# A new order of the same instructions on every engine: gateloop attention and squared-ReLU FFN

## Chip, cores, metric

One NeuronCore of a Trainium2 chip. The metric is the device time of one execution in microseconds (us). A "profile" is one recorded execution; its span leaves out about 1.8 us of the device time. In the profiles PE is the matrix engine, DVE the vector engine, ACT the scalar engine and POOL the general one; SP issues most DMA transfers (394 of 400 in the profile before). A "q" behind a name (SPq) is that engine's sequencer. The granted clock is what the profile records as PE's clock, as a share of the full one (1.00 is full).

## The reference, cut to what matters

```
for t in range(S):                              # S = 768 steps, 4 batches x 8 heads, head size 48
    new_re = ar * S_re - ai * S_im              # complex gate, |a| limited to 0.999
    new_im = ar * S_im + ai * S_re
    kv = np.einsum('bhd,bhe->bhde', k[:, :, t], v[:, :, t])
    S_re, S_im = (new_re + kv, new_im)
    y[:, :, t] = np.einsum('bhd,bhde->bhe', q[:, :, t], S_re)
...
h = np.maximum(x @ w_in, 0.0)                   # x: 3072 x 384, w_in: 384 x 2048
return (h * h @ w_out).astype(np.float32)       # w_out: 2048 x 384, weights given in float64
```

## The kernel before

The tokens are worked off in 12 groups of 256 (two chunks, a and b, of 128). A group's gates become products on DVE and ACT ("o" steps), PE makes scores, values and states from them ("a" and "b" steps), and two matrix products follow ("F", then "T" or "Z"). The float64 weights are decoded on DVE ("D" steps). The whole order is written down by hand in one string; DVE, PE, SP and ACT are given their instructions in the order in which the string names the steps (in the profile DVE stood still for 2.91 us before the second mask of group 1, at 122.20 us, and D10, which the string puts next on DVE, began behind it at 123.34 us):

```
    work = {
        "o": lambda gi, k: operands_of[gi][k](),
        "a": lambda gi, k: chunks_of[gi][0][k](),
        "b": lambda gi, k: chunks_of[gi][1][k](),
        "g": fill_gaps,
        "F": first_product,
        ...
        "T": block_of_second,
        "E": end_of_second,
        ...
        "s": store,
        "f": fetch,
        "D": weights,
        ...
        "l": load_parts,
        "v": load_values,
    }
    ...
    by_hand = {mybir.EngineType.DVE, mybir.EngineType.PE, mybir.EngineType.SP,
               mybir.EngineType.Activation}
    with tc.manual_schedule(engines=by_hand):
        follow(FRONT)
```

The second product of group 0 sums in two tiles of the pool `py`, the one of group 1 in a tile of the pool `pa`:

```
    ffn = ctx.enter_context(tc.tile_pool(name="ffn", bufs=2))
    pa = ctx.enter_context(tc.tile_pool(name="pa", bufs=1, space=PSUM))
    py = ctx.enter_context(tc.tile_pool(name="py", bufs=2, space=PSUM))
    ...
    def block_of_second(i, f):
        if f == 0:
            if i:
                both = pa.tile([C, HH, NP, C], F32, tag="a", name="o_ps").rearrange(
                    "p b x t -> p (b x t)")
            for b in range(GC):
                o_of[i, b] = both[:, b, 0:DM] if i else py.tile([P, DM], F32, tag="y", name="o_ps")
        for b in range(GC):
            second_product(i, b, [f])
```

The results are copied to output tiles (`bufs=2` of `ffn`), and stored:

```
    def end_of_second(i, b):
        out_of[i, b] = ffn.tile([P, DM], F32, name="o")
        nc.scalar.copy(out=out_of[i, b], in_=o_of[i, b])

    def store(i, b):
        nc.sync.dma_start(out=in_turn(out, groups[i][b]), in_=out_of[i, b])
```

And the scores of the next group take the same `py` and `pa` tiles again, so they cannot start before those copies are done:

```
        def scores():
            ...
            ys = tiles["y"] = [py.tile([P, NP, C], F32, tag="y", name="y") for _ in range(2)]
            ps = tiles["ps"] = pa.tile([C, HH, NP, C], F32, tag="a", name="a_ps")
```

## Time and profile before

| | before |
|---|---|
| median of the first 3 runs | 707.13 us (706.68 to 709.1) |
| PE starts its unbroken run (T0.0) | 125.7 us |
| end of the products of groups 0 and 1 | 188.5 us |
| first product of group 2 starts (F2.0) | 204.6 us |
| last matmul ends / span of the profile | 699.4 / 706.7 us |

Up to T0.0 DVE decides, later PE: from 72 to 102 us DVE is busy for 28.8 of 30 us, from 126 to 189 PE for 63.0 of 63. Between 188.5 and 204.6 us, called the hole below, PE has no bulk work: group 1's products are done and group 2's scores, masks and values must come first. The chain of waits of the kernel before over the hole (start us, length us, what), with the small pieces left out, reads

```profile
188.47 0.33 PE tp L866 x3
188.80 1.03 PE y L851 x32
189.83 2.01 PE a_ps L859 x32
...
191.86 1.23 DVE a L478
...
198.81 1.15 DVE a L478
...
202.28 2.21 DMA x<-x
```

The state products and the scores (PE y, then PE a_ps) follow on the products within 0.4 us, the two masks (DVE a) are 7 us apart, and the hole ends with a small DMA on which F2.0 waits.

### The profile page before, as it was taken

Reading aid. Unit: us, or ns where it says so; the run is one execution under the profiler, and the core shown is the slowest. Engines: PE = TensorE matmul, PEld = TensorE weight load, DVE = VectorE, ACT = ScalarE, POOL = GpSimd, SP = SyncE. Lnnn points to the kernel's source line nnn. Section 1 sums busy time; section 2 is a strip of 40 time slices with the busy share of each in tenths; the row PEclk is TensorE's granted clock in tenths of the full one; section 3 lists DMA queues with packets and bytes.
Section 4 is the critical chain, followed back from the end, with each engine's and each line's share of the span. In section 5 each row is a group of like instructions: output and inputs, shape, how many; then the busy total and the mean of one; then the engine's idle time right before and its main releaser. Section 6 shows DMA issues by size and latency. Waiting matters only on the chain.

```text
span 706.7 us, 12470 instructions
## 1 busy us (share of the span) xinstructions
PE 625.0 (88%) x4955; PEld 549.8 (78%) x4955; DVE 523.9 (74%) x916; ACT 380.6 (54%) x684; POOL 13.0 (2%) x49
## 2 busy tenths in 40 slices
PE   0007859999989999999999999999999999999995
PEld 0006638776668998988989989988989988999895
DVE  3999997979898697786696795895885975972130
ACT  6547684583636745646547458357258267350330
POOL 3000000000000000000000000000000000000000
PEclk9999977999999999999999999999999999999998
DMA  6678853505207016017034152161161170110101
GB/s 163 133 123 141 144 130 102 178 19 89 68 30 110 5 29 135 2 51 112 26 75 64 32 101 34 41 102 22 41 107 18 45 108 13 30 22 2 29 1 28
DMA packets 46148, 47.75 MB, mean 68 GB/s; under 512 B 6016, under 2 KB 40960, under 8 KB 46080
## 3 DMA queue, kind: packets, MB, share of 16 engines
q1 hardware_dynamic: 45600, 46.46, 33.6%
q8 instruction: 41, 0.67, 0.4%
q10 hardware_dynamic: 480, 0.39, 0.2%
q14 instruction: 27, 0.22, 0.1%
HBM read 36.18 MB, written 4.72 MB: 58 GB/s over the span
## 4 chain that ended last, share of the span: by engine, by line
PE 73%; DVE 13%; DMA 7%; ACT 2%; SPq 2%; issue 1%; DVEq 0%
PE h_ps L939 27%; PE o_ps L1016 23%; PE a_ps L859 6%; PE o_ps L955 6%; DVE pr L478 3%; PE y L851 3%; PE y L885 3%; DMA raw<-in_feat_dram 3%; DVE ab L478 3%; PE add L903 2%; PE tp L866 2%; DMA words<-in_moe_w_in_dram 2%; DMA vt<-in_vtok_dram 2%; SPq L815 2%; DVE room L478 1%
## 5 line engine op out<-in xcount | busy, mean ns | idle before, releaser
L939 PE MATMUL h_ps<-x,w 128*128 128x256 f32 x1152 | 258.1, 383 | 4.8 <-DMA x<-x 2.7
L939 PEld LDWEIGHTS h_ps<-x,w 128*128 128x128 f32 x1152 | 219.5, 192 | 36.4 <-ACT h L944 3.3
L944 ACT ACTIVATE h<-h_ps 128x512 f32<-128x512 f32 x96 | 57.5, 599 | 130.3 <-PE h_ps L939 127.6
L1016 PE MATMUL o_ps<-w,h 128*128 128x192 f32 x640 | 110.6, 329 | 0.0
L1016 PEld LDWEIGHTS o_ps<-w,h 128*128 128x128 f32 x640 | 103.6, 190 | 1.6 <-issue 0.5
L478 DVE TENSOR_TENSOR pr<-ab 128x384 f32<-128x384 f32 (+2 forms) x168 | 66.4, 413 | 6.0 <-ACT ab L743 1.7
L478 DVE TENSOR_TENSOR a<-a_ps,mask 128x1024 f32<-128x1024 f32 x24 | 29.4, 1224 | 54.8 <-PE a_ps L859 54.6
L866 PE MATMUL tp<-ident,qk 128*128 128x128 f32 x120 | 22.5, 300 | 50.0 <-DVE qk L478 34.9
L945 ACT ACTIVATE h<-h 128x512 f32<-128x512 f32 x96 | 60.6, 631 | 3.0
L866 PEld LDWEIGHTS tp<-ident,qk 128*128 128x128 f32 x120 | 14.8, 150 | 56.6 <-issue 37.2
L1016 PE MATMUL o_ps<-w_sum,mix 128*128 128x192 f32 x320 | 56.0, 329 | 0.0
L478 DVE TENSOR_TENSOR mix<-h 128x256 f32<-128x256 f32 x40 | 16.9, 422 | 48.2 <-ACT h L945 47.9
L1016 PEld LDWEIGHTS o_ps<-w_sum,mix 128*128 128x128 f32 x320 | 51.6, 190 | 1.1 <-issue 0.5
L478 DVE TENSOR_TENSOR ab<-pr 128x192 f32<-128x192 f32 (+1 forms) x180 | 45.8, 277 | 4.6
L478 DVE TENSOR_TENSOR qk<-ab,qk 128x768 f32<-128x768 f32 x48 | 44.9, 956 | 0.9
L669 ACT ACTIVATE qk<-raw 128x768 f32<-128x768 f32 x24 | 36.8, 1534 | 10.6 <-DMA raw<-in_feat_dram 6.5
L955 PE MATMUL o_ps<-w,h 128*128 128x384 f32 x128 | 42.2, 487 | 0.3 <-ACT x L894 0.3
L859 PE MATMUL a_ps<-qk 48*128 48x128 f32 x576 | 41.3, 293 | 0.0
L859 PEld LDWEIGHTS a_ps<-qk 48*128 48x128 f32 x576 | 36.5, 199 | 4.6 <-issue 4.2
L669 ACT ACTIVATE ab<-raw 128x768 f32<-128x768 f32 x24 | 35.7, 1577 | 2.4 <-DVE qk L478 2.4
L955 PEld LDWEIGHTS o_ps<-w,h 128*128 128x128 f32 x128 | 24.2, 190 | 16.3 <-ACT x L894 0.5
L669 ACT ACTIVATE room<-z 128x768 f32<-128x768 f32 x24 | 36.5, 1555 | 0.0
(103 smaller groups left out, 790.4 us busy)
## 6 DMA issues: line engine op xcount, KB each, us to landing
raw<-in_feat_dram SPq DMA_DIRECT2D x44, 288.0 KB
words<-in_moe_w_out_dram SPq DMA_DIRECT2D x8, 768.0 KB
last<-qk SPq DMA_DIRECT2D x72, 64.5 KB
vt<-in_vtok_dram SPq DMA_DIRECT2D x24, 192.0 KB
out_dram<-o SPq DMA_DIRECT2D x24, 192.0 KB
raw<-in_feat_dram SPq DMA_DIRECT2D x132, 32.0 KB
words<-in_moe_w_in_dram SPq DMA_DIRECT2D x16, 192.0 KB
words<-in_moe_w_in_dram SPq DMA_DIRECT2D x32, 96.0 KB
```

Source lines behind the costliest of these rows:

```text
L478: nc.vector.tensor_tensor(out=out, in0=in0, in1=in1, op=op)
L669: nc.scalar.activation(out=out.rearrange("p c j n -> p c n j"), func=AF.Copy, in_=in_.rearrange("p c (n j) -> p c n j", j=L), **kwargs)
L815: nc.sync.dma_start(out=last[gi % 2][at, :, :, 0:C + 1], in_=qk[pads(hh), :, :, g, 0:C + 1])
L851: nc.tensor.matmul(ys[p_ % 2][crossed(hh, p_), p_ // 2], lhsT=states[b][1 - c_seq % 2][rows(hh), c, p_], rhs=operand(c, p_, rows(hh)), sta ...
L859: nc.tensor.matmul(ps[:, hh, p_], lhsT=operand(2 + c, p_, rows(hh)), rhs=operand(c, p_, rows(hh)), start=(c == RE), stop=(c == IM))
L866: nc.tensor.transpose(tp[:, g], operands[gi][:, 2 + c, b, g, 0:C], ident)
L885: nc.tensor.matmul(tiles["y"][p_ % 2][crossed(hh, p_), p_ // 2], lhsT=v[:, at:at + ROWS], rhs=tiles["am"][:, hh, p_], start=(first and p_ ...
L939: nc.tensor.matmul(ps[:, j], lhsT=w1[:, g, (2 * f + j) * P:(2 * f + j + 1) * P], rhs=x_of[i][:, g], start=(g == 0), stop=(g == NG - 1))
L944: nc.scalar.activation(out=h, in_=h_ps[i, f], func=AF.Relu)
L945: nc.scalar.activation(out=h, in_=h, func=AF.Square)
L955: nc.tensor.matmul(o_of[i, b], lhsT=tokens_of(i, f, b)[:, j], rhs=w2[:, k], start=(k == 0), stop=(k == NFB - 1))
L1016: nc.tensor.matmul(to, lhsT=x(k)[:, j], rhs=factor(z)[:, 2 * k + j], start=(z in (0, 1, 3) and k == j == 0), stop=(k == KH // 2 - 1 and j ...
```

## The change

The order string was replaced by one that a longer search over a replay of the kernel had found, with two steps' durations corrected in that replay. The same 1082 steps stand in both strings and the tiles are the same. The diff is the string alone. Its lines around the end of the products of groups 0 and 1, the rest cut:

```diff
     FRONT = (
-        "l0.0 M0 v1 f0 v0 o0.0 l0.1 o0.3 o0.1 o0.4 o0.5 o0.7 o0.2 M1 D0 f1 o0.10 o0.8 o0.9 "
-        "o0.11 W0 o0.6 o0.12 o0.15 o0.22 f2 W1 o0.13 o0.16 o0.14 l1 W2 o0.17 D1 o0.18 f3 o0.19 "
...
-        "l3 o2.16 F1.7 T1.0 H1.7 o2.17 T1.1 D15 o2.18 T1.2 o2.19 T1.3 T0.7 o3.6 o2.20 o3.0 T1.4 "
-        "E0.0 E0.1 s0.0 s0.1 o3.3 o3.1 a2.1 o2.21 T1.5 t0 o3.4 o3.2 t1 T1.6 o3.5 t2 a2.2 T1.7 "
-        "o3.7 o3.10 a2.3 t3 E1.0 E1.1 s1.0 a2.0 o3.8 s1.1 o3.9 a2.5 a2.4 a2.6 o3.11 a2.8 a2.7 "
...
+        "l0.0 M0 v0 v1 f0 o0.0 l0.1 o0.3 o0.1 o0.4 o0.5 o0.7 o0.2 M1 o0.8 D0 f1 o0.9 o0.10 W0 "
+        "o0.11 o0.6 o0.22 D1 f2 o0.12 W1 o0.13 o0.15 o0.14 f3 W2 l1 o0.16 o0.17 W3 D2 f4 o0.18 "
...
+        "D14 o3.1 o3.2 T1.5 o3.4 D15 a2.2 T0.6 o3.5 a2.3 T1.6 a2.4 t0 t1 T1.7 t2 T0.7 E1.0 o3.7 "
+        "E1.1 s1.0 s1.1 o3.10 a2.8 t3 E0.0 E0.1 s0.0 a2.0 o3.8 s0.1 a2.9 o3.9 b2.1 a2.5 b2.2 "
...
```

After, group 1's come first, group 0's last block T0.7 is the last product of all, and E0 stands right before the scores a2.0.

## The prediction

> **What bounds the kernel now.** I read the page first: busy time of each engine, then the 40 slices.
>
> ```profile
> span 706.7 us, 12470 instructions
> PE 625.0 (88%) x4955; PEld 549.8 (78%) x4955; DVE 523.9 (74%) x916; ACT 380.6 (54%) x684; POOL 13.0 (2%) x49
> ...
> PE   0007859999989999999999999999999999999995
> ...
> DVE  3999997979898697786696795895885975972130
> ```
>
> PE is the largest user, but the first ten slices (17.7 us each) belong to DVE: PE starts late and has holes while DVE is at 9. From slice 12 on PE is full. So the kernel has two regimes. To find the border I cut the span into windows at places where PE's work changes (columns: window, length, busy us and instructions of PE, PEld, DVE, ACT, POOL, granted clock, DMA share, GB/s).
>
> ```profile
> 0.00:48.00 48.00, 0.47 (x1) 0.18 (x1) 34.47 (x59) 25.72 (x39) 6.80 (x25) 1.00 0.73 148
> 48.00:72.00 24.00, 16.16 (x172) 13.66 (x172) 23.41 (x29) 18.82 (x35) 0.51 (x2) 0.93 0.68 118
> 72.00:102.00 30.00, 19.41 (x85) 15.59 (x85) 28.82 (x51) 20.65 (x38) 0.00 (x0) 0.95 0.69 148
> 102.00:120.00 18.00, 16.53 (x165) 13.59 (x165) 15.72 (x21) 8.99 (x20) 0.52 (x2) 0.61 0.42 111
> ...
> 126.00:189.00 63.00, 62.99 (x239) 43.05 (x241) 57.49 (x81) 36.57 (x63) 0.58 (x2) 1.00 0.38 93
> 189.00:205.00 16.00, 11.41 (x231) 9.96 (x224) 13.34 (x21) 8.63 (x18) 0.00 (x0) 0.99 0.12 36
> 205.00:700.00 495.00, 493.01 (x3990) 449.49 (x3989) 346.96 (x655) 258.35 (x467) 4.61 (x18) 1.00 0.27 50
> ```
>
> Three things are to be seen. From 126 to 189 and from 205 to 700 us PE is busy without a hole; between them it misses 4.6 us. A busy PE need not be a fast one, so I took the spacing of matmul ends from the chain of waits: 216 ns for a 256-column one, 162.5 ns for 192 columns, 322 ns for 384, 62 ns for the scores (a_ps), and so on. Those spacings times the counts make 495 us minus 8.9 us for the last stretch: PE runs at its own pace there, and what it loses is mostly 0.2 us each time it goes from the 48- or 64-row matmuls to the full ones. True waits in that stretch are in PE's own list of waits from 204 us on:
>
> ```profile
> PE y L851 <- DMA last<-qk: 1.4, 2, 0.9
> PE h_ps L939 <- DMA x<-x: 1.2, 1, 1.2
> ```
>
> Third, PE begins its unbroken run at 125.67 us, with the first second-product block of group 0 (T0.0):
>
> ```profile
> 125.67 8.01 PE o_ps L955 x24
> 133.68 12.95 PE h_ps L939 x60
> ```
>
> All that PE does later is fixed in amount. So the end is: the start of T0.0, plus fixed matmul time, plus the hole at 189 to 205, plus the few waits, plus the 7 us tail (last copy and store). A new order of the same instructions can only move the first, third and fourth term.
>
> [...]PE idled 7.26 us before 102, the granted clock in 102 to 120 was 0.61, and 24 score matmuls took 2.94 us there and 1.61 us at 120. [...]DVE sat still 2.91 us before one masking step (scores not ready) with a weight decode standing behind it. [...]
>
> **The change, part by part.** The plan has the same 1082 steps before and after; nothing is added or removed, 911 DVE instructions are the same. So I add DVE durations along both orders, since DVE leads until T0.0. From the groups by form: a decode D is 0.558+0.959+0.563+0.959+0.958 = 4.00 us; a group's operand steps (o) sum to 27.7 us; a mask (a.5, b.5) 1.22; a state update 1.7 to 2.2. In the order before, the last operand step of group 1 (o1.20) ends at DVE sum 87.4, and the trace has it at 100.0: DVE had lost 12.6 us to waits, nearly all before 23.4 us, and then ran without a gap. Sums of the two orders, in us:
>
> - o0.20 (operands of group 0 ready): 35.7 before, 39.7 after, as decode D1 now stands before it.
> - o1.20 (group 1): 87.4 before, 81.1 after, as D4 to D7 are moved behind.
> - second mask of group 1 (b1.5), which opens T0.0: 106.7 before, 102.7 after.
> - D15, the last decode: 151.1 before, 160.6 after.
>
> So DVE work ahead of T0.0 shrinks by 4.0 us. Against it stand costs that the sums do not show:
>
> (a) The value loads v0 now go ahead of the first weights f0: two more issues of about 0.75 us, so D0, which already waited 1.30 us for f0, starts about 1.5 us later. (b) D1 now stands right after o0.11, at DVE sum 10.5, or about 24 us. Its words landed only about 27.2 us (ACT's first reader of them, L590, started at 27.25 after waiting 2.59 us for that DMA). DVE therefore stands until 27.2 or so, where before it went on at 23.4: a loss of up to 3.8 us, (a) included; 2.5 to 3.8 as SP may issue a little earlier. (c) PE comes to group 0's scores cold and now does the state sums (add, 1.95 us cold) first; b0.5 then stands behind the scores (3.8 us cold), and I count 0 to 2 us of DVE waiting. Sum: 4.0 - 3.2 - 1.0 = about 0, within -2 to +1.5.
>
> PE's own chain tells the same stretch from the other side. In the new order F0.5 waits for D5, whose sum is 85.1; with 12.6 + 3.2 + 1.0 of waits it ends at 102. After it PE must do, in order, F0.5 to F0.7 (3 x 2.6), a1's scores 3.0, its sums 1.1 and values 1.0, b1's scores 3.0, mask 1.2, values and sums 2.1, four to five transposes 1.5: about 20.5 us warm, so T0.0 at 122.5; with the clock at half for part of it 2 to 4 us more. I take 123.7 against 125.67: **2.0 us gained**.
>
> From T0.0 to the end of group 0 and 1's products PE has 62.6 us of work in either order (96 x 0.216 + 128 x 0.322 + 0.7). The later decodes (D12 to D15 end near 156 to 177 us) come before PE needs them in the new order, since the blocks that need them were moved back too. No gain, no loss.
>
> The hole at 189 to 205: before, from the end of the products to F2.0 it took 15.9 us. The new order puts the state update a2.9 ahead of the mask a2.5, so 2.2 us of DVE leave the path between the two masks; it puts the sums a2.8 (1.1 us) ahead of the scores, onto the path. New sum: 1.1 + scores 3.0 + mask 1.25 + gate step o3.11 3.6 + mask 1.2 + values 0.9 + copies 0.7 + issue 0.7 + x landing 2.25 + 0.3 = 15.0: **0.9 gained**.
>
> Steady groups: PE had 8.9 us above its spacings there. The switches from narrow to full matmuls are about as many (28 instead of 30, and six more before transposes at 0.15, six more pairs saving 0.15): nothing to speak of. The waits on last<-qk (2.0 us of extra time at two places) may go, as the search had them in view; I count 1.2. Something for the groups 3 to 5, whose order is new and irregular: 0.5.
>
> Sum: 2.0 + 0.9 + 1.2 + 0.5 = 4.6 us; I add 1 us because the order was chosen by a search that saw more than my sums. 707.1 - 5.6 = **701.5 us**.
>
> **The rivals.** First, *the front gains its full 4 to 8 us*: if the words of D1 land sooner than I think, or the corrected durations were just those of the loads, DVE stands less and T0.0 comes at 118 to 120. For it speaks that o1.20 is 6.3 us earlier in the sums; against it the 27.25 us of L590. Then 696 to 698. Second, *a new wait eats the gain*: D1 on its DMA, PE falling to half clock while it waits for D5 to D7, scores cold. For it speaks the 0.61 clock at 102 to 120[...]. Then 704 to 708. Third, *a steady group got a bubble* of half a us, some eight times over: 4 us lost. Against it: PE was full in all of these groups, and DVE has 11 us or more of room in each (347 of 495 us busy).
>
> **Range and chances.** Even with every wait after 125 us gone (about 9 us of the 8.9 and 6.9 can be reached, as switches stay) and T0.0 at 117 the time is about 692, so over 2% faster (below 693) needs everything at once: 0.05. Over 2% slower would need 14 us of new holes: 0.02. The middle eight tenths: 696.0 to 707.0.
>
> **What would show it.** In the changed profile: D1 (second L577 on DVE) idle before it on words, right at 27 us; o1.20 near 97 to 99; T0.0 (first L955) at 121 to 126; F2.0 at 198 to 204; from there to the end of PE within 3 us of the 494.8 of before; the same tail of 7 us. I am wrong if T0.0 comes before 119, or if the stretch after F2.0 changes by more than 4 us.

## More of the kernel before

Before, group 0's copies and stores (E0, s0) stand well ahead of group 1's (E1, s1).

## The result, and the profile after

| | before | after |
|---|---|---|
| median of 6 runs | 709.22 us (706.68 to 709.54) | 716.12 us (714.19 to 718.26) |
| ratio, 95% interval | | 1.0107 (1.0081 to 1.0133) |
| T0.0 / end of products / F2.0 | 125.7 / 188.5 / 204.6 us | 126.0 / 189.0 / 211.7 us |
| last matmul ends / span | 699.4 / 706.7 us | 705.5 / 712.8 us |

A ratio is the mean time of the one kernel's fast runs over that of the other's of the same rounds, so it is not quite the ratio of the medians. The change made the kernel 1% slower, where 701.5 us had been predicted. The page of the kernel after:

```profile
PE   0005489999979999999999999999999999999995
...
PEclk9999689999869999999999999999999999999998
```

Slices 11 and 12 (178 to 214 us) show 9 and 7 in the PE row where the kernel before has 9 and 8, and the granted clock falls to 8 and 6 there. By windows (same columns as in the prediction; the borders are moved to this kernel's own stages):

```profile
126.00:189.00 63.00, 63.00 (x238) 43.06 (x234) 60.92 (x87) 38.91 (x70) 0.48 (x2) 1.00 0.45 103
189.00:212.00 23.00, 16.47 (x231) 13.85 (x232) 14.98 (x20) 9.18 (x18) 0.00 (x0) 0.72 0.18 55
212.00:706.00 494.00, 493.33 (x3990) 448.85 (x3989) 347.34 (x656) 262.38 (x466) 3.56 (x18) 1.00 0.25 49
```

The stretch from 126 to 189 is as full as before. The hole has grown from 16 to 23 us and has a mean clock of 0.72. From 212 on PE is full again, and its one wait on other work in that stretch, the second line here, is down to 0.2 us (the first line is the wait that ends the hole):

```profile
PE h_ps L939 <- DMA x<-x: 4.3, 1, 4.3
PE y L851 <- DMA last<-qk: 0.2, 1, 0.2
```

So the 6.1 us between the two profiled spans are: +0.5 up to the end of the products (189.0 against 188.5), **+6.6 in the hole** (22.8 us from there to F2.0 against 16.2), -1.0 from F2.0 to the last matmul (493.8 against 494.8), 0.0 in the tail (7.3 both). The chain of waits of the kernel after through the hole:

```profile
186.42 0.87 ACT o L977 x2
187.29 0.32 SPq L980
...
187.71 3.58 DMA out_dram<-o
...
191.39 0.49 ACT o L977
...
191.92 1.63 PE y L851 x30
193.55 3.74 PE a_ps L859 x32
...
197.31 1.24 DVE a L478
...
205.05 1.24 DVE a L478
...
207.47 0.65 SPq L510
...
208.92 2.69 DMA x<-x
```

The copies E1 fill both output tiles at 186.4 to 187.3; the second of the two stores takes 3.58 us to land; only then does ACT make the last copy of group 0's results (191.39, the one before it at 190.41), and only then are the tiles free that the scores need. The same scores (a_ps x32) took 2.01 us before and take 3.74 us here. ACT's list of waits between 180 and 220 us names the stores, which stand nowhere in that of the kernel before:

```profile
ACT o L977 <- DMA out_dram<-o: 1.2, 2, 0.7
```

Only 1.2 us of ACT's time are charged to it, as ACT did another step meanwhile (0.85 us from 188.90); that it costs far more on PE needs the clock. Windows inside the hole of the kernel after, then of the kernel before:

```profile
186.00:192.00 6.00, 4.54 (x48) 2.70 (x50) 5.86 (x7) 2.80 (x6) 0.00 (x0) 1.00 0.22 66
192.00:203.00 11.00, 10.50 (x118) 8.71 (x118) 5.41 (x6) 5.63 (x10) 0.00 (x0) 0.53 0.16 46
```

```profile
190.00:205.00 15.00, 10.41 (x199) 9.13 (x198) 12.62 (x20) 7.63 (x16) 0.00 (x0) 0.99 0.13 38
```

After the wait PE ran at about half rate for 10 us, in which it looks busy (10.50 of 11 us) and does 118 matmuls; the kernel before kept the full clock through its hole. It lost it right behind, though: cut by single microseconds, its clock is at half from 204.6 to 208.0 us, so its first product of group 2 starts at half rate. The kernel after falls a second time there, from 209.4 to 216.2 us. Windows around F2.0, before and then after:

```profile
205.00:208.00 3.00, 3.00 (x8) 2.37 (x8) 2.76 (x10) 0.00 (x0) 0.00 (x0) 0.50 0.35 117
```

```profile
209.00:217.00 8.00, 5.26 (x14) 4.32 (x15) 7.65 (x14) 1.90 (x3) 0.00 (x0) 0.57 0.33 79
```

### The profile page after: what moved, and what is told of

It is laid out like the page before. It is cut to its first block, busy times and chain, and to the rows that moved or that the text cites.

```text
span 712.8 us, 12462 instructions
## 1 busy us (share of the span) xinstructions
PE 623.8 (88%) x4955; PEld 548.6 (77%) x4955; DVE 524.8 (74%) x916; ACT 385.5 (54%) x684; POOL 12.4 (2%) x49
## 4 chain that ended last, share of the span: by engine, by line
PE 80%; DVE 8%; DMA 6%; SPq 3%; issue 1%; ACT 1%; DVEq 0%; ACTq 0%
PE h_ps L939 32%; PE o_ps L1016 26%; PE a_ps L859 6%; PE o_ps L955 5%; PE y L885 3%; PE y L851 3%; DMA words<-in_moe_w_in_dram 3%; PE add L903 2%; PE tp L866 2%; DMA raw<-in_feat_dram 2%; DVE qk L478 1%; DVE ab L478 1%; DVE room L478 1%; SPq L815 1%; DVE pr L478 1%
## 5 line engine op out<-in xcount | busy, mean ns | idle before, releaser
L939 PEld LDWEIGHTS h_ps<-x,w 128*128 128x128 f32 x1152 | 221.9, 194 | 45.4 <-issue 14.1
L669 ACT ACTIVATE ab<-raw 128x768 f32<-128x768 f32 x24 | 37.2, 1560 | 5.9 <-DVE qk L478 5.9
L478 DVE TENSOR_TENSOR room<-ab,carry 128x1344 f32<-128x1344 f32 x24 | 36.3, 1552 | 2.2 <-ACT carry L784 2.2
```

The costliest lines, as they stand in the source:

```text
L478: nc.vector.tensor_tensor(out=out, in0=in0, in1=in1, op=op)
L669: nc.scalar.activation(out=out.rearrange("p c j n -> p c n j"), func=AF.Copy, in_=in_.rearrange("p c (n j) -> p c n j", j=L), **kwargs)
L939: nc.tensor.matmul(ps[:, j], lhsT=w1[:, g, (2 * f + j) * P:(2 * f + j + 1) * P], rhs=x_of[i][:, g], start=(g == 0), stop=(g == NG - 1))
```

## The experiments

**Theory "stores, then clock"**: the new order of the output copies makes the scores of group 2 wait for a store to land, since there are two output tiles; the pause lets the clock drop to half, and that multiplies its price. Rivals: the state sums moved ahead of the scores are the cost; the front is worse than T0.0 shows; the steady groups are worse. Each ratio below is against the kernel before in the same rounds (11 of its runs each time, 6 for the change). The runs come from several sessions on several chips, in which the kernel before had medians of 707.6 to 709.2 us, so ratios are to be compared and not medians: the change cost 1.07%, or 7.6 us. "Hole" is from the end of the products to F2.0 in the one profiled execution, and T0.0 is read there too.

| run | median us | ratio (95%) | T0.0 | hole |
|---|---|---|---|---|
| the change | 716.12 | 1.0107 (1.0081 to 1.0133) | 126.0 | 22.8 |
| e1: four output tiles | 709.34 | 1.0011 (0.998 to 1.0042) | 126.4 | 17.9 |
| e9: order of the copies undone | 709.97 | 1.0024 (0.9992 to 1.0056) | 126.4 | 17.3 |
| e5: PE kept at work | 709.33 | 1.0032 (1.001 to 1.0054) | 127.9 | 19.0 |
| e4: before, copies swapped | 716.3 (5 fast runs) | 1.0125 (1.0088 to 1.0162) | 125.9 | 29.2 |
| e2: front of after, rest of before | 711.85 | 1.0052 (1.0021 to 1.0084) | 125.4 | 16.2 |
| e3: up to F2.0 of before, rest of after | 706.33 | 0.9974 (0.9947 to 1.0002) | 125.4 | 16.2 |
| e6: e1, DMA order | 707.17 | 1.0002 (0.9981 to 1.0023) | 126.5 | 16.7 |
| e7: e1, D1 later | 706.31 | 0.9993 (0.9971 to 1.0015) | 123.1 | 17.3 |
| e8: e3 with four tiles, PE kept at work | 707.31 | 0.9998 (0.9973 to 1.0023) | 125.7 | 17.3 |
| c1: e7, two gap copies first, PE kept at work | 705.62 | 0.9967 (0.9935 to 0.9998) | 124.3 | 16.7 |
| c2: c1, PE kept at work once more | 704.99 | 0.9953 (0.9921 to 0.9985) | 125.3 | 16.6 |

All were correct.

### e1: four output tiles

```diff
-        out_of[i, b] = ffn.tile([P, DM], F32, name="o")
+        out_of[i, b] = ffn.tile([P, DM], F32, name="o", bufs=4)
```
(at both places that make this tile)

> The changed kernel with four output tiles instead of two, so that no copy of an output waits for an earlier store to land. Theory 'stores' (the new order of the four output copies of groups 0 and 1 puts two stores and the score matmuls of group 2 into one line): the two waits of ACT on the stores go, scores of group 2 end near 194 us instead of 197.3, and group 2's first product starts 3 us or more earlier than 211.7; time about 711 to 713, more if the clock then stays full (709). Rival 'sums first' (the state sums moved ahead of the scores, and cold clock, are the cost): only some 1 to 2 us are gained, and the scores still end after 196; time 714 to 716.

Measured 709.34 us, a ratio of 1.0011: about 6.8 of the 7.6 us that the change had cost are gone with a wait that the list of waits puts at 1.2 us. The chain through the hole, and the window of the former half rate:

```profile
190.53 1.48 PE y L851 x32
192.00 2.01 PE a_ps L859 x32
194.04 1.24 DVE a L478
```

```profile
192.00:203.00 11.00, 9.34 (x167) 7.98 (x166) 8.60 (x12) 6.38 (x14) 0.00 (x0) 1.00 0.17 53
```

The scores begin 1.5 us sooner than in the kernel after and are back at 2.01 us, and the clock stays whole up to 206.4 us. There it falls to half for 6.8 us (0.55 from 207 to 214), while PE waits 4.7 us for x and then begins F2.0; e9 has the same slow start (the first 44 matmuls of group 2's first product take 12.66 us there, 45 take 12.94 in e1). The state sums are still ahead of the scores, so the rival "sums first" is out as the main cost.

### e4: the one thing put into the kernel before

```diff
-... T1.4 E0.0 E0.1 s0.0 s0.1 o3.3 ... a2.3 t3 E1.0 E1.1 s1.0 a2.0 o3.8 s1.1 ...
+... T1.4 o3.3 ... a2.3 t3 E1.0 E1.1 s1.0 s1.1 E0.0 E0.1 s0.0 a2.0 s0.1 o3.8 ...
```

> The kernel before with one thing of the change: the output copies and stores of group 0 moved behind those of group 1 (the order E1.0, E1.1, stores, E0.0, E0.1, store). Theory 'stores': group 2's scores now wait for two stores to land (their tiles are those of the copies they wait for), so ACT waits on stores appear, scores end 3 to 4 us later than 191.8, and the time rises by 3 to 6 us (712 to 715)[...]. Rival 'sums first': nothing moves by more than 1 us.

The five fast runs have a median of 716.3 us and a ratio of 1.0125, which can't be told from the 1.0107 of the change: the swap alone costs as much as the whole new order. The direction was right and the expected size a little too small. The profile is of the slowest of the five (725.66 us), so its hole of 29.2 us is longer than is usual for this run. In it the clock was at half from 194.3 us to beyond F2.0 (0.60 over the whole hole). ACT's waits in the hole, and the chain:

```profile
ACT o L977 <- DMA out_dram<-o: 3.8, 2, 3.1
```

```profile
194.75 1.98 PE y L851 x30
196.73 3.74 PE a_ps L859 x32
...
207.34 3.74 PE a_ps L859 x32
```

Both score blocks of group 2 run at 3.74 us. The sixth run took 3655.83 us; it is slow and not used, and why is left open (the kernel has a second, general path for inputs out of range, and whether this execution took it was not looked at).

### e9: the one thing taken back from the change

```diff
-... T0.6 o3.5 a2.3 T1.6 a2.4 t0 t1 T1.7 t2 T0.7 E1.0 o3.7 E1.1 s1.0 s1.1 o3.10 a2.8 t3 E0.0 E0.1 s0.0 a2.0 o3.8 s0.1 a2.9 ...
+... T0.6 o3.5 a2.3 T0.7 E0.0 E0.1 s0.0 s0.1 T1.6 a2.4 t0 t1 T1.7 t2 E1.0 o3.7 E1.1 s1.0 s1.1 o3.10 a2.8 t3 a2.0 o3.8 a2.9 ...
```

> The changed kernel with two output tiles and one thing undone: group 0's last second-product block, its two output copies and its stores stand ahead of group 1's last two blocks again, so the stores of group 0 land while PE still has 5 us of products to do. Theory 'stores, then clock': ACT no longer waits for a store (or under 0.5 us), the scores of group 2 end near 193 to 194, with no half-rate clock from 192 to 203, group 2's first product near 206 to 208; time 709 to 711 against 716 of the changed kernel. Rival 'the search's front or steady groups hold the loss': 714 or more.

Measured 709.97 us, a ratio of 1.0024, as expected. With two tiles and no other edit, moving five steps out of 1082 gives back about 5.9 of the 7.6 us. ACT has no wait on a store in its list any more, and the mean clock in the hole is 0.98.

### e5: the wait left in, the clock held up

```diff
+    def keep_warm(i, n):
+        ps = ph.tile([P, 2, TOK], F32, tag="h", name="warm")
+        for _ in range(n):
+            nc.tensor.matmul(ps[:, 0], lhsT=w1[:, 0, 0:P], rhs=w1[:, 0, 0:TOK], start=True, stop=True)
-... s0.0 a2.0 ...          -... F2.0 ...
+... s0.0 P2.4 a2.0 ...     +... P3.6 F2.0 ...
```

> The changed kernel with matmuls that nobody reads, only to keep PE at work where it waits in the hole: 4 (1.7 us) ahead of group 2's scores, 6 (2.6 us) ahead of group 2's first product. Theory 'the clock is a large part of the hole': the granted clock stays full from 192 to 203, the scores end 2 us earlier though 1.7 us of work was added, values and second scores are faster by 2 us, the first product starts warm; time 3 to 5 us below the changed kernel (711 to 713). Rival 'the clock is a side effect of the wait and costs little': time 716 to 717.

Measured 709.33 us, a ratio of 1.0032 where the change had 1.0107: about 5.3 us gained, a little better than expected. The wait on the stores is still there (1.2 us in ACT's list), and more work was added:

```profile
193.00:204.00 11.00, 10.15 (x186) 8.48 (x185) 7.31 (x8) 7.32 (x13) 0.00 (x0) 1.00 0.19 55
```

The clock is full where it was 0.53, and 186 matmuls fit in the 11 us where 118 did. The hole went from 22.8 to 19.0 us though the wait stayed, so about 3.8 of the 6.6 us that it had grown are paid in clock; by e1, e4 and e9 the slow clock comes with the wait (mean clock in the hole 0.60 in e4, which has it, and 0.98 in e1 and e9, which don't). The other part of the gain lies behind the hole: the second lot of matmuls lets F2.0 start at full clock (1.00 from 204 to 217 us), which it doesn't in the kernel before either (0.50 from 205 to 208), and from F2.0 to the last matmul e5 takes 492.1 us against 493.8. The two lots were not run apart. The gains of e1 and e5 together are more than the loss: both remove the same slow stretch, each in its own way; no run has both.

### e2 and e3: which part of the order costs

> The changed kernel's order up to the first second-product block of group 0 (T0.0), the order before from there on. Theory 'hole': the front is a tie (T0.0 at 126.0 against 125.7), so T0.0 comes at 126 and the rest is as before: group 2's first product near 205, time within 2 us of the kernel before (708 to 711). Rival 'the front costs more than T0.0 shows' (decodes D9 to D15 end later in the new front and are missed afterwards): holes on PE between 126 and 189, time 712 or more.

> The order before up to group 2's first product (F2.0), the changed order from there on. Theory 'hole': the changed order of the steady groups is a little better (7.3 us above the matmul spacings instead of 8.9, waits on the last heads gone), so the time is 1 to 2 us below the kernel before: 707 to 708.5, ratio 0.997 to 0.999. Rival 'steady groups cost too': ratio over 1.002.

e3 came out as expected by its ratio (0.9974; 706.33 us): the new order of the steady groups may be worth 1 to 2 us, but the interval takes in 1, so a gain is not shown. It is no loss that could explain the change. e2 is 711.85 us, a little over what I expected. Its hole is 16.2 us, as in the kernel before, which clears the front of the big loss. But the rival had a point: from T0.0 to the end of the products PE took 64.9 us, 62.8 and 63.0 in the two originals. It waited 0.9 us there for a decode that the new front puts later (w) and 0.9 us for operands (qk). And in its profile the clock dropped again at 588 to 595 us (0.83 from 580 to 600), after a wait of 1.3 us on last<-qk. Splicing two orders makes a third, whose seams have costs of their own.

### e6 and e7: where the promised 4 us of the front went

e6, on top of e1: `v0` behind `f0`, `v2` behind `g0`, `v4` behind `g2`. e7, on top of e1:

```diff
-... o0.11 o0.6 o0.22 D1 f2 o0.12 W1 o0.13 o0.15 o0.14 ...
+... o0.11 o0.6 o0.22 f2 o0.12 W1 o0.13 o0.15 D1 o0.14 ...
```

> Four output tiles as in e1, and three things of the change undone in the DMA queue: the first value loads behind the first weights (v0 after f0), and the loads v2 and v4 behind the gap copies g0 and g2. Theory: D0 waits about 1.3 us instead of 3.8, but D1 then waits longer for its words, which land at the same time, so DVE gains nothing from v0; the first product of group 0 starts 2 us earlier than 85.4 (worth nothing, as it waits for D5 later), that of group 2 about 1 us earlier than 207.2; time 708 to 709 (e1: 709.3). Rival 'the queue order is half of the front': T0.0 at 124 or sooner, time under 707.

> Four output tiles as in e1, and the decode D1 moved one step back on DVE, behind the first half of the gate products (o0.15), so that its words have landed when DVE comes to it. Theory: the 3.6 us that DVE stood before D1 go; the operands of group 1 are ready near 97 instead of 100.3, T0.0 at 123 to 124 instead of 126.4, time 706 to 707. Rival 'DVE's wait is given back on PE' (clock, DMA of x): T0.0 stays at 126, time 709.

DVE's list of waits up to 130 us has these two lines in the kernel after, where the kernel before has one, of 1.3 us:

```profile
DVE decoded L577 <- DMA raw<-in_feat_dram: 3.8, 1, 3.8
DVE decoded L577 <- DMA words<-in_moe_w_in_dram: 3.6, 1, 3.6
```

They are D0 and D1. In e6 D0 waits 1.2 us and D1 then 5.2. The words of D1 did not land at the same time, as the theory had it: D1 starts at 27.3 us, 29.3 in e1. But DVE gave these 2 us back: up to 130 us it waited 4.7 us for PE's scores, 2.8 in e1, and T0.0 stays at 126.5. The gap copies gained what was expected (F2.0 at 206.1); in time the difference from e1 is inside the intervals. In e7 the wait before D1 is gone:

```profile
32.10 0.56 DVE L577 TENSOR_SCALAR decoded<-words 128x768 int32<-128x768 int32 x1
```

and group 1's operands are ready at 96.8 us (100.3 in e1) and T0.0 comes at 123.1 (126.4). In the profiles the 3 us stay up to F2.0 (203.4 against 207.2 us). In time they are not shown: the ratio of 0.9993 is only 1.3 us below that of e1, the intervals overlap, and the profile is of the fastest of the six runs of e7. One decode moved behind o0.15 recovers, in this profile, most of the gain that the front had on paper.

### e8, c1 and c2: a version that beats both?

> The order before up to group 2's first product and the changed order after it (as e3, 706.3), with four output tiles and with matmuls that nobody reads in two waits of PE: 14 (6 us) ahead of group 1's first transpose, where PE idled 7.3 us and fell to half clock from 99 to 116, and 4 (1.7 us) ahead of group 2's first product. If the clock costs there: group 1's scores take 2.0 instead of 3.7 us, T0.0 comes 2 to 4 us before 125.4, the first product of group 2 starts warm; time 702 to 704. Rival: DVE bounds that stretch anyway, time 706.

e8 missed: 707.31 us. With the extra matmuls the clock was full up to 105 us (1.00 from 95 to 105, 0.69 in the kernel before), but it then fell all the same, from 105 to 116 (0.53), over the narrow matmuls of group 1's states and scores; the first scores ended at 111.6 us, no sooner than without them (110.8 in e3). With the matmuls ahead of it F2.0 came later (205.8 us, 204.4 in e3).

> The changed order with what the runs found: four output tiles (e1), D1 one step later (e7), the gap copies g0 and g2 ahead of the loads v2 and v4 (part of e6), 4 matmuls that nobody reads (1.7 us) ahead of group 2's first product (as in e8). If the gains add: T0.0 at 123, group 2's first product at 202.5 and warm, time 703 to 705, under the kernel before by 0.4 to 0.7%. If they don't: 706, as e7.

> As c1_best, and 6 more matmuls that nobody reads (2.6 us) ahead of F0.5, where PE waits for the decode D5 and then ran at half clock from 101 to 104. If the clock costs there: T0.0 1.5 to 2 us sooner than in c1_best, time 701 to 703. If DVE (D8, the masks) bounds T0.0 by then: as c1_best.

c1 is 705.62 us and c2 704.99. Both are below the kernel before (intervals under 1) and about 1.4 to 1.5% below the change; a difference between c1 and c2 is not shown. c1 came between its two expectations, and c2 missed the gain: T0.0 did not move forward in its profile (125.3, 124.3 in c1). The added matmuls began only at 100.5 us, at half clock, and took 4.5 us instead of 2.6, so that F0.5 started at 104.9 us where it had started at 102.2 in c1. Of the 2.7 us by which F0.5 was later, 1.0 was left at T0.0.

## Why the prediction was wrong

Its frame held, but for matmul times that stretch when the clock falls (a_ps x32 from 2.01 to 3.74 us): the end is the start of T0.0, plus matmul time, plus the hole, plus few waits, plus a 7 us tail. One term of the sum broke.

- **The step that failed** is "New sum: 1.1 + scores 3.0 + mask 1.25 + gate step o3.11 3.6 + mask 1.2 + values 0.9 + copies 0.7 + issue 0.7 + x landing 2.25 + 0.3 = 15.0: 0.9 gained". Measured: 22.8 us, 6.6 lost (against 16.2 before, counted from the end of the last product; the prediction has 15.9). The sum follows only the new order's matmuls and DVE steps. It takes the scores to be free to start when their turn comes. They needed the tiles of E0, E0 needed an output tile, and the tile needed a store to land: 3.58 us on the chain. I had the swap of E0 and E1 before me in the diff and did not ask which buffers the copies write to. e1, e4 and e9 show it from three sides.
- The same sum used 3.0 us for state products and scores and 0.9 for values. At half rate they were 5.4 and 2.0. My second rival, "a new wait eats the gain", with PE falling to half clock, was the right mechanism, in the wrong place (the front) and at 704 to 708 instead of 716. e5 shows that the clock is the larger part of the price in the hole (about 3.8 of 6.6 us).
- x landing: 2.69 us, and 0.65 us for the load v4 that the new order puts ahead of the gap copy; my 2.25 and 0.7 left that out. That is why the hole is still 17.9 us in e1, without the wait on the store, and not 15.0. e6 gets about 1 us back.
- **Front**: 2.0 us gained was predicted, 0.3 lost measured (T0.0 at 126.0, inside the 121 to 126 that I named). The 2.0 stood against both of its own workings: the DVE side gave "about 0", and the PE side 122.5 plus 2 to 4 us of half clock, so 124.5 to 126.5. The DVE sums were right (99.9 us at the end of o1.20, less 18.5 us of waits, is 81.4; 81.1 was summed); group 1's operands came at 99.9 against 97 to 99. The mis-sized terms are (a), 3.8 us of waiting for D0's words instead of 1.30 + 1.5, and (b), D1's words at 28.9 us instead of 27.2. In the profile of e7 D1's place is worth 3 us at T0.0.
- From T0.0 to the end of the products "no gain, no loss": 63.0 us against 62.8. Right.
- Steady groups: 1.2 + 0.5 us gained was predicted, 1.0 measured in the profiles, the waits on last<-qk gone but for 0.2. The mechanism was right and the size somewhat too large; e3 does not speak against it.
- "I add 1 us because the order was chosen by a search": no run supports it. Whether the replay knew of the store or of the clock cannot be told from these runs.

## What to carry to other kernels

When an order changes, list for each moved step not only what it reads but which buffers it takes and who must let go of them: a copy that writes to a rotating tile inherits the landing of the store before it, here 3.58 us. Price a new PE pause ahead of narrow matmuls with the clock in view: here about 1.5 us of pause on PE (0.91 and 0.55) was followed by a granted clock of 0.53 over 11 us, and came with a loss of 7. And before trusting a searched order, undo the few steps around its longest new wait one by one: one more pair of buffers (e1), or five steps in 1082 (e9), gave back most of the difference.

## What these runs leave open

- What brings the clock down. In the kernel after it fell at 192 us though PE's longest pause in the hole until then was 0.91 us, and it stayed down while PE looked busy for 10.50 of 11 us, mostly with narrow matmuls. In the kernel before, with pauses of up to 1.34 us between such matmuls, it stayed up to 204.6 us. These runs don't give a length or a share at which short pauses bring it down, or show what counts as a pause in narrow matmuls.
- How long a store takes. The stores of 192 KB that ACT waited for took 3.58 us on the chain of the kernel after and 3.77 us on that of e4; what sets this time was not looked at.
